# Last inverse stage through ScalarE, shift weights by broadcast, coarser units and a new order in a fused Hyena-like block

## The chip, the cores and the metric

The kernel runs on one core of a Trainium2 chip. Five engines work side by side, each through its own queue in the order in which the program was written: TensorE (PE; its weight loads are shown as PEld), VectorE (DVE), ScalarE (ACT), GpSimd (POOL) and SyncE (SP), which here only issues DMAs. The metric is device time in microseconds (us); lower is better.

## The reference

For 2048 positions of 640 channels the block computes a normalisation, a gated long convolution and a feed-forward net, and joins them:

```python
xn = _layernorm(x)                       # x is A_q, [2048, 640]
k_shift = sum(k_pad[t:t+S] * shift_k[:, 3-t] for t in range(4))
kv = k_shift * v
y = irfft(rfft(kv, 2S) * rfft(ssm_k, 2S))[:S] + kv * ssm_D
s = xn * y
h = gelu(xn @ w1 + b1)                   # 640 -> 1728
g = silu(h @ w2 + b2)                    # 1728 -> 640
out = x + s * g
```

## The kernel before

The 2048 positions lie as 128 partitions by 16 tiles of 640 channels (x, xn, k, v). The convolution is done as a two-stage transform by matmuls, with its results passed through three scratch tensors in DRAM, which turn rows into columns between the stages:

- Forward stage 1 (`stage1`, operations K1, K1r, U1, U1r): the filter K = ssm_k and the signal U = kv, tile by tile, times a table W. `Ke`, `Ker`, `Ue`, `Uer` evict PSUM to a staging buffer `st` of four slots, and `Ks`, `Us` store each slot to scrK or scrU.
- Forward stage 2, in eight groups s: `KLs`, `ULs` load a group from scrK and scrU, K2, U2 and X2 (X2 does the last 128 channels of both) transform it, `Kf`, `Uf` evict, `pr` and `qr` multiply the two spectra.
- Inverse stage 1: `i1`, `i1r`, evicted by `ie`, `ier`, stored to scrC by `cs_0` to `cs_7`.
- Inverse stage 2: `cl_0` to `cl_7` load from scrC (each once all stores are in), `i2_i` makes tile i of y.

The signal comes from the shift convolution `kv` on VectorE: five pieces of rows, each four multiplications with a spread weight row, three additions and one product with v. The spread weights `wx` (4 × 640 values on all 128 partitions) are made in the head.

The feed-forward net runs in four quarters c of four tiles. Each tile is normalised (`bn` statistics, `ep` and `rs` for the reciprocal root, `xn`), then transposed: `xt` on TensorE with eviction `xe` for quarters 0 and 1, a DMA transpose `xT` for 2 and 3. `f1_c_ft_r` makes 128 hidden features for piece r of the quarter, and `ge` applies Gelu while evicting; `f1h`, `geh` do the last 64 features. `f2_i_n` makes half n of tile i's output, `si` evicts it through Silu, `gx` multiplies it into xn. At the end `ym` multiplies y in, `ad` adds x, and `os` stores.

Nothing is scheduled on the chip. `ORDER` is a list of all operations by name; `plan.emit` records them in that order, so it sets the order in every engine's queue. Behind a name, `/P`, `/S`, `/D`, `/A` pick POOL, SP, DVE or ACT where there is a choice, `/C` splits a matmul into two halves of 64 output columns, and the numbers behind a colon are buffer slots: PSUM banks (eight), slots of `st`, and the 11 row blocks of the tile kvl in which the loads of the second stages land. An operation waits until its slot's earlier user is done.

Warm-up matmuls (`warm`) fill TensorE in the head before the first data.

Of the kernel before, what the change touches and what calls it, by code (L numbers as in the profile page):

```python
# [112 lines left out]
def h3_block(ctx: ExitStack, tc: tile.TileContext, x_d, k_d, v_d, sk_d, K_d, D_d, w1_d, b1_d, w2_d, out_d):  # L113
# [33 lines left out]
    ones = sb.tile([1, P], BF16, name="ones")  # L147
# [12 lines left out]
    sk_r = lat_t[0:1, 0:4, :].rearrange("p a d -> p (a d)")  # L160
# [17 lines left out]
    def evict(e, out_, in_):  # L178
        (nc.scalar.copy if e == "ACT" else nc.vector.tensor_copy)(out=out_, in_=in_)  # L179
# [12 lines left out]
    def pair():  # L192
        return Buf(pool=ps, size=2)
# [15 lines left out]
    Fb, Ib, idb, b1b, b1rb, Db, cb, tmb, smb, skb, zb, mhb = (Buf() for _ in range(12))  # L209
# [100 lines left out]
    def load(name, eng, o_, i_, reads=(), writes=()):  # L310
        op(name, eng, lambda e: qu(e).dma_start(out=o_, in_=i_), reads=reads, writes=writes)
# [18 lines left out]
    load("skl", "ACT", sk_r, sk_d, writes=[skb])  # L330
    for j in range(4):
        pb = pair()

        def wx_mm(e, j=j, pb=pb):
            for h in range(2):
                nc.tensor.matmul(out=pb.v[:, h, 0:H], lhsT=ones[:], rhs=sk_r[:, j * D + h * H:j * D + (h + 1) * H],
                                 start=True, stop=True)
# [50 lines left out]
    LG = ((0,), (1,), (2, 3)) + tuple(tuple(range(4 * c, 4 * c + 4)) for c in range(1, NCH))  # L388

    def bn(e, i):  # L390
        for h in range(2):
            nc.vector.bn_stats(out=stats[:, i, h, :], in_=x_t[:, i, h * H:(h + 1) * H])  # L392
        nc.vector.bn_aggr(out=mv[:, i, :], in_=stats[:, i, :, :])
# [8 lines left out]
    for g, tiles in enumerate(LG):  # L402
        for i in tiles:
            op("bn%d" % i, "DVE", lambda e, i=i: bn(e, i), reads=[xb[i]], writes=[mvb[i]])
# [112 lines left out]
    kt = Pool(2, lambda s, n: kvt_t[s], after=[[skb]] * 2)  # L517
# [20 lines left out]
    for i in range(8):  # L538
# [3 lines left out]
              after=[kv_done[0:(2, 3, 4, 5)[m]] for m in range(4)] + [vb[4 * m:4 * m + 4] for m in range(4)] + [acc + wxb + [skb]] * 3)  # L542
    pm = Pool(5, lambda s, n: st_t[:, s * 4 * CA:(s + 1) * 4 * CA], after=[stored] * 5)
    rest = None
    for s in range(NG):
# [41 lines left out]
        prb = [Buf(pool=pm), Buf(pool=pm)]  # L587
        for w in range(2):
# [23 lines left out]
        if s % 2 == 0:  # L612
            rest = dict(b=Buf(pool=pm), p=[Buf() for _ in range(4)], U=[], C=[], s=[])
# [41 lines left out]

    for r in range(NG):
# [3 lines left out]
        for i in (2 * r, 2 * r + 1):  # L660
            pb = pair()

            def i2(e, i=i, b=cb_, pb=pb):
# [6 lines left out]
            op("ym_%d" % i, "DVE", lambda e, i=i, pb=pb: nc.vector.tensor_tensor(  # L670
                out=xn_t[:, i, :], in0=pb.v.rearrange("p a b -> p (a b)")[:, 0:D], in1=xn_t[:, i, :], op=ALU.mult), reads=[pb], writes=xnb[i])
            if i >= FLIP:
                continue
            op("ad_%d" % i, "DVE", lambda e, i=i: nc.vector.tensor_tensor(  # L674
                out=x_t[:, i, :], in0=xn_t[:, i, :], in1=x_t[:, i, :], op=ALU.add), reads=xnb[i], writes=[xb[i]])
            op("os_%d" % i, "SP|ACT", lambda e, i=i: qu(e).dma_start(out=out_d[:, i, :], in_=x_t[:, i, :]), reads=[xb[i]])
# [117 lines left out]
```

## Time and profile before

| what | us |
|---|---|
| median of 3 runs (185.93 to 187.03) | 186.15 |
| the profiled execution | 186.39 |
| its span, first to last instruction | 184.6 |
| TensorE busy | 176.7 |
| VectorE busy | 156.5 |
| ScalarE busy | 144.2 |
| GpSimd busy | 15.3 |

The profile is of one execution, whose own time is 1.8 us longer than its span. Rows of groups read: line, engine, operation, output<-input by the program's names, shapes, count, busy time, mean ns of one. Rows of the timeline and of the chain begin with the start in us and the length. "SPq" or "ACTq" is an engine's queue issuing a DMA. The tile name of an eviction is its output, ps is PSUM.

### The profile page before, as it was taken

To read this page: it belongs to the slowest core of one execution; us is meant where nothing else is said; L and a number is where in the kernel's file an instruction comes from. 1 tells how busy PE (TensorE), PEld (TensorE's weight loads), DVE (VectorE), ACT (ScalarE), POOL (GpSimd) and SP (SyncE) were. 2 spreads that over 40 slices of the span, in tenths; PEclk is the share of its full clock that TensorE was granted. 3 is DMA by queue.
4 is the path that set the end of the run, shared out by engine and by line. 5 is a ranking of instruction groups with operands and counts; after the bars stand their busy time and mean duration, and the time that the engine had idled before them with its cause. 6 is when DMAs were issued, how large, how long until landed. Compare 5 with 4: busy or idle time off the path is not lost.

```text
span 184.6 us, 5181 instructions
## 1 busy us (share of the span) xinstructions
PE 176.7 (96%) x2182; PEld 102.6 (56%) x2183; DVE 156.5 (85%) x267; ACT 144.2 (78%) x227; POOL 15.3 (8%) x42
## 2 busy tenths in 40 slices
PE   7998999999999999998999999999999999899991
PEld 2335784547666556664553435544564555588870
DVE  7999999999999999919999969958889730689993
ACT  4898989999999999987859897898797897501120
POOL 2458600000000000020020000000000000000000
PEclk9999999999999999999999999999999999999999
DMA  5999999959879995989989760899923756995275
GB/s 182 411 417 413 401 417 417 431 223 344 305 274 312 401 396 217 385 253 374 220 261 326 135 162 4 260 376 189 362 74 122 265 185 215 388 344 227 77 270 194
DMA packets 29754, 51.81 MB, mean 281 GB/s; under 512 B 9122, under 2 KB 23843, under 8 KB 29348
## 3 DMA queue, kind: packets, MB, share of 16 engines
q1 hardware_dynamic: 28288, 50.21, 78.7%
q10 hardware_dynamic: 1444, 1.28, 2.1%
q8 instruction: 17, 0.28, 0.6%
q14 instruction: 5, 0.04, 0.1%
HBM read 31.30 MB, written 18.35 MB: 269 GB/s over the span
## 4 chain that ended last, share of the span: by engine, by line
PE 71%; DVE 12%; DMA 12%; ACT 3%; issue 1%; ACTq 0%; SPq 0%; DVEq 0%
PE ps L450 32%; PE ps L486 20%; PE ps L603 5%; PE ps L560 4%; PE ps L358 4%; DMA kvl<-scrC 4%; DVE stats L392 3%; DVE xn L670 3%; DMA kvl<-scrU 2%; DMA scrU<-st 2%; DMA x<-in_x 2%; ACT st L179 2%; PE ps L464 1%; PE ps L635 1%; PE ps L574 1%; DVE x L674 1%
## 5 line engine op out<-in xcount | busy, mean ns | idle before, releaser
L486 PE MATMUL ps<-w,hT 128*128 128x320 bf16 (+4 forms) x588 | 66.1, 295 | 0.0
L450 PE MATMUL ps<-xnT,w 128*128 128x512 bf16 (+5 forms) x515 | 62.2, 321 | 0.1
L486 PEld LDWEIGHTS <-hT 128*128 128x128 bf16 (+2 forms) x588 | 45.1, 103 | 19.8 <-issue 6.5
L179 ACT CAST kvl<-ps 128x1024 bf16<-128x1024 f32 (+3 forms) x53 | 42.1, 841 | 8.2 <-PE ps L560 5.1
L450 PEld LDWEIGHTS <-w 128*64 128x64 bf16 (+1 forms) x515 | 32.1, 105 | 25.1 <-issue 7.8
L454 ACT ACTIVATE hT<-ps,b1f 128x512 bf16<-128x512 f32 (+2 forms) x71 | 37.8, 591 | 3.3 <-PE ps L450 3.1
L179 ACT CAST st<-ps 128x1024 bf16<-128x1024 f32 (+1 forms) x45 | 37.8, 902 | 1.3 <-PE ps L358 1.1
L179 DVE CAST kvl<-ps 128x1024 bf16<-128x1024 f32 (+2 forms) x31 | 25.9, 857 | 7.1 <-ACT hT L454 2.3
L490 ACT ACTIVATE sl<-ps 128x320 bf16<-128x320 f32 (+1 forms) x33 | 14.0, 438 | 20.7 <-PE ps L486 14.6
L670 DVE TENSOR_TENSOR xn<-ps,xn 128x640 bf16<-128x640 f32 x16 | 12.8, 819 | 9.5 <-PE ps L666 9.4
L593 DVE TENSOR_TENSOR st<-kvl 128x2048 bf16<-128x2048 bf16 x16 | 19.1, 1217 | 0.3 <-ACT kvl L179 0.3
L531 DVE TENSOR_TENSOR kvl<-kvl 128x2560 bf16<-128x2560 bf16 (+1 forms) x15 | 18.3, 1223 | 0.4
L528 DVE TENSOR_TENSOR kvl<-kvl 128x2560 bf16<-128x2560 bf16 (+1 forms) x15 | 18.3, 1221 | 0.3
L392 DVE BATCH_NORM_STATS2 stats<-x 128x6 f32<-128x320 bf16 x32 | 13.7, 471 | 4.0 <-DMA x<-in_x 4.0
L697 PE MATMUL ps<-hT 128*128 128x512 bf16 x31 | 9.8, 461 | 1.4 <-DVE hT L223 1.3
L492 DVE TENSOR_TENSOR xn<-xn,sl 128x320 bf16<-128x320 bf16 (+1 forms) x33 | 9.8, 309 | 0.8 <-ACT sl L490 0.8
L560 PE MATMUL ps<-kvl,F 64*32 64x512 bf16 x256 | 10.1, 381 | 0.0
L408 POOL TENSOR_TENSOR rstd<-rstd,mhalf 128x4 f32<-128x4 f32 (+2 forms) x6 | 5.0, 838 | 57.1 <-DVE rstd L406 56.8
L603 PE MATMUL ps<-st,I 32*64 32x512 bf16 x256 | 8.9, 380 | 0.0
L624 DVE TENSOR_TENSOR st<-kvl 128x512 bf16<-128x512 bf16 x16 | 6.5, 416 | 0.8 <-ACT kvl L179 0.8
L666 PE MATMUL ps<-kvl,G 128*64 128x512 bf16 (+1 forms) x64 | 6.1, 301 | 1.0 <-DVE x L674 0.5
L697 PEld LDWEIGHTS <-hT 128*128 128x128 bf16 x32 | 3.1, 111 | 6.3 <-issue 3.2
(76 smaller groups left out, 124.4 us busy)
## 6 DMA issues: line engine op xcount, KB each, us to landing
scrK<-st SPq DMA_DIRECT2D x8, 640.0 KB, 5.2
scrU<-st SPq DMA_DIRECT2D x8, 640.0 KB, 4.5
kvl<-scrK SPq DMA_DIRECT2D x8, 640.0 KB, 6.9
kvl<-scrU SPq DMA_DIRECT2D x8, 640.0 KB, 5.7
scrC<-kvl SPq DMA_DIRECT2D x8, 640.0 KB, 4.0
kvl<-scrC SPq DMA_DIRECT2D x8, 640.0 KB, 7.6
kvl<-in_v SPq DMA_DIRECT2D x4, 640.0 KB, 11.5
w<-in_w SPq DMA_DIRECT2D x2, 1120.0 KB, 8.3
```

The costliest lines, as they stand in the source:

```text
L179: (nc.scalar.copy if e == "ACT" else nc.vector.tensor_copy)(out=out_, in_=in_)
L392: nc.vector.bn_stats(out=stats[:, i, h, :], in_=x_t[:, i, h * H:(h + 1) * H])
L450: nc.tensor.matmul(out=pb.v[us, 0:n], lhsT=w1_t[:, ft, t, us], rhs=xnTb[c].v[:, a:b, t, :], start=(t == 0), stop=(t == DT - 1))
L454: nc.scalar.activation(out=hTb[c].v[:, ft, a * P:b * P], in_=pb.v[:, 0:(b - a) * P], func=ACT.Gelu_apprx_tanh, bias=b1_f[:, ft:ft + 1], sc ...
L486: nc.tensor.matmul(out=pb.v[w * u:w * u + w, 0:b - a], lhsT=hTb[c].v[0:M, ft, q * P + w * u:q * P + w * u + w], rhs=w2_t[0:M, ft, a:b], st ...
L490: op("si_%d_%d" % (i, n), "ACT", lambda e, pb=pb, s_=s_, a=a, b=b: nc.scalar.activation(out=s_.v[:, 0:b - a], in_=pb.v[:, 0:b - a], func=A ...
L528: op("kv%d_%dm" % (r, j), "DVE", lambda e, i=i, n=n, j=j, t=t, wb=wb: nc.vector.tensor_tensor(out=t.v[:, 0:n, :], in0=k_t[:, i + 3 - j:i + ...
L531: op("kv%d_%da" % (r, j), "DVE", lambda e, n=n, t=t, a=a: nc.vector.tensor_tensor(out=a.v[:, 0:n, :], in0=a.v[:, 0:n, :], in1=t.v[:, 0:n, ...
L560: nc.tensor.matmul(out=pb.v[32 * j:32 * j + 32, a, :], lhsT=F2_t[64 * a:64 * a + 64, ri, :], rhs=B.v[64 * a:64 * a + 64, j, 0:CA], start=T ...
L593: nc.vector.tensor_tensor(out=pr.v.rearrange("p (a r c) -> p a r c", a=2, r=2), in0=u, in1=k, op=ALU.mult)
L603: nc.tensor.matmul(out=pb[j // 2].v[64 * a:64 * a + 64, j % 2, :], lhsT=I1_t[32 * j:32 * j + 32, m, :], rhs=o[32 * j:32 * j + 32, a, r, :] ...
L670: op("ym_%d" % i, "DVE", lambda e, i=i, pb=pb: nc.vector.tensor_tensor(out=xn_t[:, i, :], in0=pb.v.rearrange("p a b -> p (a b)")[:, 0:D], ...
```

## The change

Five things change, and with them the whole order.

1. Last inverse stage: `ym` no longer reads PSUM. `ye_i` evicts tile i to a new bf16 buffer `yt` (in the space of `st`, free once all products are used), 13 of the 16 on ScalarE and 3 on VectorE; `ym`, and for the first 12 tiles `ad` and `os`, then work on two tiles at once.
2. Shift weights: the 5 KB load, four pairs of matmuls with a row of ones and four evictions go; one DMA `wl` on SP reads the row once for each of 128 partitions into `wx`.
3. Statistics: `bn` does two tiles, the four half-tile statistics first and the two aggregations behind them. The loads of x in the head become tiles 4-5, 6-7 and 0-3 (the last is issued first).
4. Gelu units: quarter 0 goes from 32 pieces to 13 whole units, quarter 1 from 13 whole units to 7 whole and 12 halves.
5. All eight `cs` stores to scrC are on GpSimd's queue (`/P`) instead of SP's.

```diff
-    for g, (a, b) in enumerate(((0, 1), (1, 2), (2, 4), (4, 8))):
+    for g, (a, b) in enumerate(((4, 6), (6, 8), (0, 4))):
         load("xl%d" % g, "SP", x_t[:, a:b, :], x_d[:, a:b, :], writes=xb[a:b])
...
-    load("skl", "ACT", sk_r, sk_d, writes=[skb])
-    for j in range(4):
...
-        op("wm%d" % j, "PE", wx_mm, reads=[skb, cb], writes=[pb])
-        op("we%d" % j, "ACT|DVE", lambda e, j=j, pb=pb: evict(
-            e, wx_t[:, j, :].rearrange("p (h c) -> p h c", h=2), pb.v[:, :, 0:H]), reads=[pb], writes=[wxb[j]])
+    load("wl", "SP", wx_t[:], sk_d.to_broadcast([P, 4 * D]).rearrange("p (j d) -> p j d", d=D), writes=wxb)
...
     def bn(e, i):
-        for h in range(2):
-            nc.vector.bn_stats(out=stats[:, i, h, :], in_=x_t[:, i, h * H:(h + 1) * H])
-        nc.vector.bn_aggr(out=mv[:, i, :], in_=stats[:, i, :, :])
+        for j in range(i, i + 2):
+            for h in range(2):
+                nc.vector.bn_stats(out=stats[:, j, h, :], in_=x_t[:, j, h * H:(h + 1) * H])
+        for j in range(i, i + 2):
+            nc.vector.bn_aggr(out=mv[:, j, :], in_=stats[:, j, :, :])
...
     def pieces(c, ft):
-        if c > 0:
-            return ((0, 4),)
-        return ((0, 1), (1, 2), (2, 4)) if ft < SPLIT else ((0, 2), (2, 4))
+        return ((0, 2), (2, 4)) if c == 1 and ft < SPLIT else ((0, 4),)
...
+    yt = Pool(8, lambda s, n: st_t[:, s * 2 * D:(s + 1) * 2 * D].rearrange("p (a d) -> p a d", d=D), after=[pmb] * 8)
...
-            op("ym_%d" % i, "DVE", lambda e, i=i, pb=pb: nc.vector.tensor_tensor(
-                out=xn_t[:, i, :], in0=pb.v.rearrange("p a b -> p (a b)")[:, 0:D], in1=xn_t[:, i, :], op=ALU.mult), reads=[pb], writes=xnb[i])
...
+            op("ye_%d" % i, "ACT|DVE", lambda e, i=i, pb=pb: evict(
+                e, yb[i // 2].v[:, i % 2, :], pb.v.rearrange("p a b -> p (a b)")[:, 0:D]), reads=[pb], writes=[yp[i]], hold=[yb[i // 2]])
+        i = 2 * r
+        op("ym_%d" % i, "DVE", lambda e, i=i: nc.vector.tensor_tensor(
+            out=xn_t[:, i:i + 2, :], in0=yb[i // 2].v, in1=xn_t[:, i:i + 2, :], op=ALU.mult),
+           reads=yp[i:i + 2] + [yb[r]], writes=xnb[i] + xnb[i + 1])
...
 ORDER = """
-c0 grid xl2 b1l zz fix warm5:0 skl wq1 bn3 ws1 xl3 mh warm12:1 warm2:0 warm3:1 bn2 bn7 Kl3 bn6 warm14:0 id wm2:2 wm3:0 we2 wm0:4
...
+grid zz xl2 warm11:0 b1l fix Kl2 mh sm0 warm12:1 warm5:0 warm1:1 wq1 warm13:0 xl0 c0 bn2 bn0 ws1 warm15:1 Kl3 warm7:0 xl1 ep2/P
...
 """
```

Where the order moves work shows best on the queues. First SP's queue from the second-stage loads to the end; before:

```order
L548 DMA kvl<-scrU 128x4x640
L650 DMA scrC<-kvl 128x4x640
L548 DMA kvl<-scrU 128x4x640 x2
L547 DMA kvl<-scrK 128x4x640 x2
L496 DMA_TRANSPOSE G<-W 128x16x128
L650 DMA scrC<-kvl 128x4x640 x7
L658 DMA kvl<-scrC 128x2560 x6
L676 DMA out<-x 128x640
L658 DMA kvl<-scrC 128x2560 x2
L676 DMA out<-x 128x640 x5
```

and after the change, from the three loads UL7, UL5 and UL6 on (the two loads of scrK are KL6 and KL7):

```order
L535 DMA kvl<-scrU 128x4x640 x3
L534 DMA kvl<-scrK 128x4x640 x2
L482 DMA_TRANSPOSE G<-W 128x16x128
L650 DMA kvl<-scrC 128x2560 x8
L673 DMA out<-x 128x1280 x3
```

The eight stores to scrC (L650 before) are gone from this queue, and no output store stands between the eight loads of scrC any more. The stores are now the last work of GpSimd's queue, behind the reciprocal roots of the layer norm and the preparation of tables:

```order
L302 MEMSET hT_71 1x512
L298 TENSOR_SCALAR I_83<-I_83 128x192
L394 TENSOR_SCALAR rstd<-mv 128x4
L396 TENSOR_TENSOR rstd<-rstd,mhalf 128x4 x2
L639 DMA scrC<-kvl 128x4x640 x8
```

They left SP's queue for one that issued no DMA before.

On VectorE, the first products of the inverse stage before (ps is PSUM, sl the Silu output):

```order
L670 TENSOR_TENSOR xn<-ps,xn 128x640
L674 TENSOR_TENSOR x<-xn,x 128x640
L670 TENSOR_TENSOR xn<-ps,xn 128x640
L674 TENSOR_TENSOR x<-xn,x 128x640
L670 TENSOR_TENSOR xn<-ps,xn 128x640
L492 TENSOR_TENSOR xn<-xn,sl_80 128x320
```

and after, with the three evictions that VectorE keeps (st is the space that yt uses):

```order
L177 CAST st<-ps 128x640
L478 TENSOR_TENSOR xn<-xn,sl_78 128x320
L478 TENSOR_TENSOR xn<-xn,sl_80 128x320
L177 CAST st<-ps 128x640
L665 TENSOR_TENSOR xn<-st,xn 128x1280
L478 TENSOR_TENSOR xn<-xn,sl_79 128x320
L665 TENSOR_TENSOR xn<-st,xn 128x1280
L177 CAST st<-ps 128x640
```

The products read SBUF and are twice as wide; one in two is gone.

More of the change, by code (lines that the diff above doesn't have):

```diff
@@ L208, in h3_block @@
     Gb = [Buf() for _ in range(2)]
[L209 removed]
+    Fb, Ib, idb, b1b, b1rb, Db, cb, tmb, smb, zb, mhb = (Buf() for _ in range(11))
     wxb = [Buf() for _ in range(4)]
@@ L402, in h3_block @@
     for g, tiles in enumerate(LG):
-        for i in tiles:
-            op("bn%d" % i, "DVE", lambda e, i=i: bn(e, i), reads=[xb[i]], writes=[mvb[i]])
+        for i in tiles[::2]:
+            op("bn%d" % i, "DVE", lambda e, i=i: bn(e, i), reads=xb[i:i + 2], writes=mvb[i:i + 2])
         a, b = tiles[0], tiles[-1] + 1
@@ L612, in h3_block @@
         if s % 2 == 0:
-            rest = dict(b=Buf(pool=pm), p=[Buf() for _ in range(4)], U=[], C=[], s=[])
+            pmb.append(Buf(pool=pm))
+            rest = dict(b=pmb[-1], p=[Buf() for _ in range(4)], U=[], C=[], s=[])
         R = rest
@@ new lines @@
+ge_3_6_0 f1_3_2_0/C:1 ge_2_11_0 pr_3_1:1 ier_3/D ier_2/D gx_2_0 i1r_0:6.2 geh_3 UL6/S:4 ge_3_2_0 ier_1 ier_0 i1_0:4.0 ie_0_1
+pr_3_0:2 cs_2/P i1_3:2.6 ie_0_0/D ie_3_1/D pr_4_0:0 ie_3_0 f2_8_1:0.1 KL6/S:10 X2_5:6 U2_5_1:2 U2_5_0:4 Uf_5_2/D Kf_5_2/D si_8_1
+Uf_5_0 f2_8_0:1.0 U2_6_1:6 Uf_5_1 U2_6_0:2 si_8_0 KL7/S:3 qr_4_0:1 Uf_6_1 K2_6_1:4 pr_4_1:2 Uf_6_0 pr_5_1:3 f2_9_0:0.2 K2_6_0:2
+pr_5_0:4 si_9_0 X2_7:6 Kf_6_1 gx_9_0 Uf_7_2/D Kf_6_0 cs_1/P f2_9_1:1.2 Kf_7_2/D qr_5_1 qr_5_0 gx_8_1 i1_5:2.4 si_9_1 f1_3_10_0/C:0
```

118 lines of the change are left out of this document (54 added, 64 removed).

## Prediction

> **What bounds the kernel now.** I read the busy shares first, then the busy time of each stretch, then the chain of work that ended last, then single rows of the timeline. The first fence has the page's row of shares and four stretches of the span; a stretch's first figure is its length, and each engine's is its busy time in it.
>
> ```profile
> PE 176.7 (96%) x2182; PEld 102.6 (56%) x2183; DVE 156.5 (85%) x267; ACT 144.2 (78%) x227; POOL 15.3 (8%) x42
> 18.20:71.30 53.10, 53.10 (x546) 32.59 (x548) 52.17 (x53) 51.10 (x92) 3.48 (x7) 1.00 0.91 346
> 71.30:84.50 13.20, 12.48 (x158) 7.79 (x159) 8.97 (x25) 11.58 (x17) 1.04 (x1) 1.00 0.91 327
> 84.50:157.20 72.70, 72.58 (x1085) 37.13 (x1086) 56.74 (x91) 61.11 (x89) 1.33 (x2) 1.00 0.76 218
> 157.20:181.00 23.80, 22.38 (x289) 17.83 (x288) 21.39 (x47) 6.15 (x13) 0.00 (x0) 1.00 0.72 263
> ```
>
> TensorE has work from 18.2 to the end of the inverse stage. Up to 71.3 VectorE (52.17 of 53.10) and ScalarE (51.10) are as full; after 84.5 they have room, and after 157.2 ScalarE is nearly idle (6.15 of 23.80) while VectorE is nearly full (21.39). So a saving on VectorE counts only at the end, one on ScalarE hardly anywhere, and one on TensorE everywhere. The granted clock is 1.00 in all of them.
>
> What does a TensorE operation cost? In the chain of waits (start, length, what), groups follow each other without a gap:
>
> ```profile
> 18.19 7.90 PE ps L450 x115
> 84.91 0.43 PE ps L560 x16
> 85.35 2.01 PE ps L486 x14
> 87.36 0.56 PE ps L560 x16
> 154.25 1.90 PE ps L486 x14
> 173.67 6.86 PE L486 MATMUL ps<-w,hT 128*128 128x320 bf16 x56
> ```
>
> Fourteen matmuls of 320 columns take 1.90 beside matmuls of the same tile shape (154.25) and 2.01 between others (85.35); sixteen of the second forward stage take 0.43 behind their like and 0.56 between others. So a change of tile shape costs 0.11 to 0.13, and the rest is columns at about 2,400 a us. The first feed-forward matmul is at 18.19, the last ends at 173.67 + 6.86 = 180.53 (this row is the timeline's): 162.3. Counted from the written order by columns and 0.13 a change, the work in it is 157.6 (145.3 of columns, 95 changes), so 4.7 are waits.
>
> **TensorE's own work.** The new order has 75 changes of shape behind its first feed-forward matmul instead of 95: 20 × 0.13 = 2.6 less. Three transposes of xn now come behind that matmul (3 × 0.33 = 1.0 more) and one forward tile ahead of it (0.2 less). Feed-forward pieces of 128, 256 or 512 columns have the same columns in all. Work: 155.8, **1.8 less**. The eight matmuls that spread the shift weights lay in the head, where TensorE runs warm-up matmuls: nothing.
>
> **The head.** In the chain and the timeline, statistics, normalised tiles and transposed copies precede the matmul at 18.19; the fifth line is the page's row of GB/s, one figure for each 4.6 us.
>
> ```profile
> 4.53 0.90 DVE stats L392 x2
> 6.44 0.21 DVE mv L393
> 6.65 0.76 DVE stats L392 x2
> 13.17 1.02 DVE xn L412 x3
> GB/s 182 411 417 413 401 417 417 431 223 344 305 274 312 401 396 217 385 253 374 220 261 326 135 162 4 260 376 189 362 74 122 265 185 215 388 344 227 77 270 194
> 16.36 1.68 DVE L179 COPY xnT<-ps 128x640 bf16<-128x640 bf16 x4
> ```
>
> One tile's statistics take 0.76 + 0.21, about 1.0, and all eight come ahead of the first xn at 13.17. The first x load grows from 320 to 640 KB; at 411 GB/s that is 0.8 more, so they start at 5.3. Six tiles (three pairs; pairing saves at most the small gaps, I take 5.8) end at 11.1, three xn at 12.1, the fourth pair at 14.0, two xn 14.7, bit operations 15.2, two copies of 0.42 16.05, one small cast and the third copy 16.6. The first whole Gelu unit starts at 16.7 and not 18.19: **1.5 earlier**. The four ScalarE evictions of spread weights that go make room for two more of the copies there.
>
> Whole units also relieve ScalarE: eight Gelu evictions of 256 columns take 3.02, four of 512 take 2.42.
>
> ```profile
> 24.76 3.02 ACT L454 ACTIVATE hT<-ps,b1f 128x256 bf16<-128x256 f32 x8 [0.63 <-PE ps L450]
> 154.29 2.42 ACT L454 ACTIVATE hT<-ps,b1f 128x512 bf16<-128x512 f32 x4 [0.81 <-PE ps L450]
> ```
>
> At 0.38 and 0.60 a piece the first two quarters go from 20 × 0.38 + 12 × 0.31 (the 128s, estimated) + 13 × 0.60 = 19.1 to 20 × 0.60 + 12 × 0.38 = 16.6. These 2.5 hide behind TensorE, which is the one always busy there; I count nothing.
>
> **The shift convolution on VectorE.** It must be done before the last forward tile of U. Two rows of the timeline (first and last of its run), the group that multiplies by the Silu output, and the load of k that starts it:
>
> ```profile
> 20.27 1.47 DVE L528 TENSOR_TENSOR kvl<-kvl 128x2560 bf16<-128x2560 bf16 x1
> 71.59 0.83 DVE L533 TENSOR_TENSOR kvl<-kvl 128x1280 bf16<-128x1280 bf16 x1
> L492 DVE TENSOR_TENSOR xn<-xn,sl 128x320 bf16<-128x320 bf16 x31 | 9.3, 314 | 0.8 <-ACT sl L490 0.8
> 7.68 0.33 SPq L311 DMA_DIRECT2D kvl<-in_k  x1
> kvl<-in_k SPq DMA_DIRECT2D x1, 1120.0 KB, 9.6
> ```
>
> The run is 20.27 to 72.4, or 52.1. The new order puts eight of the multiplications in it instead of five (+0.9) and two pairs of statistics (+3.8), and has one 1.1 eviction less: 55.8 or so. It starts some 0.8 earlier, at 19.5, where TensorE's first unit is 1.5 earlier but three xn follow the copies; it ends at 75.3, plus about 1.0 for two multiplications whose Silu comes late. TensorE wants the tile at 16.7 + 59.4 (its work up to there) = 76.1. **Wait: 0.4**; before it there was none to speak of. The start also hangs on the load of k, which landed at 7.68 + 9.6 = 17.3. The broadcast load puts 640 KB ahead of it, 1.6 at 411 GB/s: 18.9, still before 19.5, with 0.6 to spare. A load that spreads one row over 128 partitions is not in the trace: it may cost nothing (if it fits into gaps) or as much as the slowest 640 KB load quoted below (12.4, k then some 4 late); I take 1.6, the rate row, as it moves the same bytes.
>
> **Stores and loads between the stages.** SP carried all eight stores of the inverse spectrum; now GpSimd's queue does, which issued no DMA in this trace, so the time from issue to landing there, L, is the unknown. Rows of issues, of single operations and of the chain:
>
> ```profile
> scrU<-st SPq DMA_DIRECT2D x8, 640.0 KB, 4.5
> kvl<-scrK SPq DMA_DIRECT2D x8, 640.0 KB, 6.9
> x<-in_ssm_k SPq DMA_DIRECT2D x2, 640.0 KB, 12.4
> L593 DVE TENSOR_TENSOR st<-kvl 128x2048 bf16<-128x2048 bf16 x16 | 19.1, 1217 | 0.3 <-ACT kvl L179 0.3
> L650 SPq DMA_DIRECT2D scrC<-kvl x8: 359/436/1151, 115.1 to 149.4; - x8
> DMA to landing us min/median/max: 3.2/4.0/6.5
> L408 POOL TENSOR_TENSOR rstd<-rstd,mhalf 128x4 f32<-128x4 f32 x3 | 3.1, 1038 | 57.0 <-DVE rstd L406 56.8
> 146.93 1.00 PE ps L603 x32
> 152.72 3.38 SPq L658 DMA_DIRECT2D kvl<-scrC  x6
> 157.24 0.41 PE ps L666 x4
> ```
>
> Bounds for L: 3.2, the fastest of these stores from SP, and 12.4, the slowest transfer of that size. It is nearest to the median store, 4.0; to it I add 1.0, the longest that one plain GpSimd instruction takes here (1038 ns): L = 5.0. Two places feel it.
> - The load KL7 now takes the buffer of the store cs_2. Behind its last eviction VectorE does one multiplication (0.3) and the product (1.2) that lets i1_3 start, so it is ready 1.5 ahead of i1_3. X2_7, which needs KL7, stands 8.9 behind i1_3's start (i1_3 1.0, three half tiles 6.0, second-stage groups 1.9). With 6.0 for KL7 (the median of such loads is 6.9, with others in flight; few are then) TensorE waits L − 4.4, at 5.0 **0.6**.
> - The last store was issued at 149.4, the loads behind it at 152.72 (3.3 later), and TensorE's first inverse matmul at 157.24 started as its load landed. The cover, from the end of i1_7 at 147.93, was 9.3 and is 9.2 now (five units and two half tiles in both orders). So TensorE waits L − 3.3, at 5.0 **1.7**.
>
> Other transfers: U1_12 takes the slot of a store of 4.5 behind 0.7 of eviction, and 3.9 of matmuls cover it: 0 to 1.3, I take **0.6**. K2_6 wants KL6 6.4 behind the product that frees its buffer (i1_3 1.0, two half tiles 4.0, second-stage groups 1.4), and such a load takes 6.9: **0.5**.
>
> [...]
>
> **The end.** The rows are the chain, SP's issues and groups by shape:
>
> ```profile
> 163.51 7.00 DMA kvl<-scrC
> 163.51 0.90 SPq L658 DMA_DIRECT2D kvl<-scrC  x2
> L670 DVE TENSOR_TENSOR xn<-ps,xn 128x640 bf16<-128x640 f32 x16 | 12.8, 819 | 9.5 <-PE ps L666 9.4
> L674 DVE TENSOR_TENSOR x<-xn,x 128x640 bf16<-128x640 bf16 x12 | 5.8, 485 | 0.1
> L179 ACT CAST kvl<-ps 128x640 bf16<-128x640 f32 x4 | 2.7, 720 | 0.5 <-PE ps L336 0.5
> L528 DVE TENSOR_TENSOR kvl<-kvl 128x1280 bf16<-128x1280 bf16 x6 | 4.9, 821 | 0.1
> ```
>
> VectorE: 16 × 0.82 + 12 × 0.49 = 19.0 becomes 8 × 0.82 + 6 × 0.82 + three evictions of about 0.85 = 14.0: 5.0 less. ScalarE gets 13 × 0.72 = 9.4, in a stretch where 17 of its 23.8 are free. The last two loads stood on SP behind an output store until 163.51 and landed 7.00 later, when TensorE waited; now all eight go first. From 157.24 to 180.53 are 23.3, of which 21.2 are work by the count above; of the 2.1 of waits I keep 0.5: **1.6 less**. From the last matmul to the end it was 184.6 − 180.5 = 4.1; VectorE now has two pair operations queued ahead of the last ones, and I take 4.5.
>
> **Sum.** 16.7 + 155.8 + 4.7 = 177.2; + 0.4 + 0.6 + 0.5 + 0.6 + 1.7 − 1.6 = 179.4; + 4.5 = 183.9 against a span of 184.6, 0.7 less. The profiled execution took 186.39, 0.24 above the median of 186.15, so I subtract from the median: **185.5**.
>
> **Rivals.**
> - **Slow stores** (slower). Place: cs_2 ahead of X2_7, and cs_7 ahead of the inverse loads. Price: 2 us per us of L above 4.4. From L = 5.3 it is slower than before, from 6.3 by over 1%; at 7.5 it gives 190.5. [...] 0.28.
> - **Cheap stores** (faster): L = 4.0 or less takes off 1.6 to 2.3, giving 183.2 to 183.9. The median row is for it. 0.24.
> - **The convolution starts late** (the broadcast load holds back k, or VectorE's longer run meets late Silu tiles): every us past 0.6 is one on the path, as U's last tile stands in front of all loads of the second stage; 1 to 4 late gives 186.5 to 189.5. 0.12.
> - That VectorE's 5.0 come off the span as such gives 180.5; the stretch's work on TensorE speaks against it, and I leave it out of the chances.
>
> **How the numbers follow.** Forecast, L from 4.4 to 5.9 and no late convolution: 184.1 to 187.3, chance 0.36. About 1%, or 1.9, is what a measurement of this kernel can tell from no change. Faster by that (under 184.3): cheap stores 0.24 and 0.04 of the forecast, 0.28. Slower (over 188.0): 0.26 of the slow stores, 0.09 of the late convolution, 0.35. Within: 0.37. The range, 182.6 to 190.5, leaves out 0.1 on either side.
>
> **What would show it.** First feed-forward matmul near 16.7; VectorE's convolution to about 76; a wait for kvl<-scrK ahead of X2_7 and for kvl<-scrC ahead of the first inverse matmul, together near 2.3; stores from GpSimd landing in about 5; no wait for kvl<-scrC in the last 20 us. I am wrong if the first matmul is at 18 or later, if stores take over 6, or if TensorE waits for ScalarE where Gelu units and forward evictions mix.

## The result, and the profile after

The changed kernel takes 193.12 us (median of 4 runs, 192.16 to 196.23); the kernel before, run beside it, 186.04. The ratio is **1.037**, 95% interval 1.027 to 1.048: 3.7% slower, where 185.5 was forecast. The profiled execution is the 196.23 one, span 194.4; it ran in a slower state that the ratio leaves out, so the accounts further below rest on a second profile of the same kernel, of an execution of 192.24.

From the page, the shares, the granted clock in 40 slices of 4.9 us, three groups and one row of DMA issues:

```profile
PE 179.1 (92%) x2166; PEld 103.7 (53%) x2166; DVE 149.5 (77%) x251; ACT 149.1 (77%) x227; POOL 21.1 (11%) x48
PEclk9999999999999999996699999999579999999996
L547 PE MATMUL ps<-kvl,F 64*32 64x512 bf16 x256 | 11.3, 409 | 2.9 <-DMA kvl<-scrU 2.9
L639 POOL DMA_DIRECT2D scrC<-kvl x8 | 6.3, 784 | 69.3 <-DMA kvl<-scrU 37.2
L561 PE MATMUL ps<-kvl,F 64*32 64x256 bf16 x128 | 3.7, 306 | 4.7 <-DMA kvl<-scrK 4.7
scrC<-kvl POOLq DMA_DIRECT2D x8, 640.0 KB, 6.1
```

TensorE's share falls from 96% to 92%, and two waits hold nearly all of its new idle time: 2.9 for a load from scrU (UL2, ahead of U2_2_0) and 4.7 for one from scrK (KL7, ahead of X2_7). In the course of each, the clock drops. TensorE's timeline at the two places:

```profile
89.58 1.05 PE L547 MATMUL ps<-kvl,F 64*32 64x512 bf16 x16 [2.89 <-DMA kvl<-scrU]
90.99 3.92 PE L472 MATMUL ps<-w,hT 128*128 128x320 bf16 x14
138.91 0.63 PE L561 MATMUL ps<-kvl,F 64*32 64x256 bf16 x16 [4.75 <-DMA kvl<-scrK]
139.48 3.91 PE L472 MATMUL ps<-w,hT 128*128 128x320 bf16 x14
```

And the two stretches of half clock, to their edges (columns as in the prediction's first fence; the figure of the clock is the third from the end):

```profile
88.84:95.67 6.83, 6.09 (x62) 2.63 (x61) 2.78 (x4) 2.71 (x4) 0.00 (x0) 0.50 0.94 269
136.62:143.45 6.83, 4.54 (x38) 2.18 (x46) 2.52 (x6) 0.02 (x1) 0.00 (x0) 0.50 0.65 100
```

Fourteen matmuls that take 2.0 elsewhere take 3.9 there. At a clock of 0.50, the 6.09 and 4.54 of busy time hold work for half as long: 3.0 and 2.3 are lost on top of the waits of 2.89 and 4.75. That is 12.9 of this execution.

What does X2_7 wait for? In the chain of waits, the store cs_2 and the load KL7, which takes its buffer, stand one behind the other, and later the last store cs_7 ahead of the inverse loads:

```profile
123.56 6.24 DMA scrC<-kvl
129.82 9.05 DMA kvl<-scrK
...
161.17 3.75 DMA scrC<-kvl
```

So the store lands 6.24 after issue and the load another 9.05 later. The last store, beside which no other queue moved anything from 161.1 to 165, takes 3.75.

### The profile page after: what moved, and what is told of

It is laid out like the page before. It is cut to its first block, busy times and chain, and to the rows that moved or that the text cites. A ratio compares the mean times of both kernels' runs of the same rounds, so it can differ in the third digit from the quotient of the medians.

```text
span 194.4 us, 5147 instructions
## 1 busy us (share of the span) xinstructions
PE 179.1 (92%) x2166; PEld 103.7 (53%) x2166; DVE 149.5 (77%) x251; ACT 149.1 (77%) x227; POOL 21.1 (11%) x48
## 3 DMA queue, kind: packets, MB, share of 16 engines
q0 software_dynamic: 1152, 5.24, 8.0%
## 4 chain that ended last, share of the span: by engine, by line
PE 66%; DMA 20%; DVE 9%; issue 2%; ACT 0%; SPq 0%; POOLq 0%; ACTq 0%
PE ps L436 25%; PE ps L472 25%; DMA scrC<-kvl 5%; DMA kvl<-scrK 5%; PE ps L344 3%; DMA kvl<-scrU 3%; DVE stats L379 3%; PE ps L591 3%; PE ps L547 3%; PE ps L658 2%; DMA x<-in_x 2%; DMA scrU<-st 2%; DMA kvl<-scrC 2%; DVE kvl L177 2%; DVE xn L400 1%
## 5 line engine op out<-in xcount | busy, mean ns | idle before, releaser
L472 PE MATMUL ps<-w,hT 128*64 128x320 bf16 (+3 forms) x714 | 69.5, 301 | 0.0
L436 PE MATMUL ps<-xnT,w 128*128 128x512 bf16 (+3 forms) x380 | 60.6, 361 | 0.0
L472 PEld LDWEIGHTS <-hT 128*64 128x64 bf16 (+2 forms) x714 | 49.7, 108 | 18.7 <-issue 6.3
L177 ACT CAST st<-ps 128x1024 bf16<-128x1024 f32 (+2 forms) x59 | 46.4, 848 | 4.9 <-PE ps L658 2.1
L177 ACT CAST kvl<-ps 128x1024 bf16<-128x1024 f32 (+2 forms) x50 | 39.4, 839 | 8.9 <-PE ps L547 6.5
L436 PEld LDWEIGHTS <-w 128*128 128x128 bf16 (+1 forms) x380 | 28.1, 103 | 28.5 <-issue 6.6
L177 DVE CAST kvl<-ps 128x512 bf16<-128x512 f32 (+2 forms) x30 | 25.8, 881 | 22.5 <-PE ps L561 6.0
L440 ACT ACTIVATE hT<-ps,b1f 128x512 bf16<-128x512 f32 (+1 forms) x58 | 34.5, 654 | 3.4 <-PE ps L436 3.0
L476 ACT ACTIVATE sl<-ps 128x320 bf16<-128x320 f32 (+1 forms) x33 | 14.0, 437 | 16.7 <-PE ps L472 14.9
L639 POOL DMA_DIRECT2D scrC<-kvl x8 | 6.3, 784 | 69.3 <-DMA kvl<-scrU 37.2
L177 DVE CAST st<-ps 128x640 bf16<-128x640 f32 (+2 forms) x5 | 4.4, 872 | 10.2 <-PE ps L658 10.2
## 6 DMA issues: line engine op xcount, KB each, us to landing
kvl<-in_v SPq DMA_DIRECT2D x4, 640.0 KB, 12.9
```

What stands on the lines that cost most here:

```text
L436: nc.tensor.matmul(out=pb.v[us, 0:n], lhsT=w1_t[:, ft, t, us], rhs=xnTb[c].v[:, a:b, t, :], start=(t == 0), stop=(t == DT - 1))
L440: nc.scalar.activation(out=hTb[c].v[:, ft, a * P:b * P], in_=pb.v[:, 0:(b - a) * P], func=ACT.Gelu_apprx_tanh, bias=b1_f[:, ft:ft + 1], sc ...
L472: nc.tensor.matmul(out=pb.v[w * u:w * u + w, 0:b - a], lhsT=hTb[c].v[0:M, ft, q * P + w * u:q * P + w * u + w], rhs=w2_t[0:M, ft, a:b], st ...
L476: op("si_%d_%d" % (i, n), "ACT", lambda e, pb=pb, s_=s_, a=a, b=b: nc.scalar.activation(out=s_.v[:, 0:b - a], in_=pb.v[:, 0:b - a], func=A ...
```

## The experiments

Each row of the table is the changed kernel with one edit, unless it says otherwise. Ratios are to the kernel before, run beside it; "KL7" is its time from issue to landing, and the wait is TensorE's at X2_7, both in the profiled execution.

| run | edit | median us | ratio (95%) | KL7 | wait |
|---|---|---|---|---|---|
| c_after | none | 192.12 | 1.035 (1.027 to 1.044) | 9.62 | 4.54 |
| e1_xt2 | xT2 behind UL1 | 195.40 | 1.050 (1.041 to 1.060) | 10.56 | 5.40 |
| e2_gt | G's transposition after KL7 | 193.87 | 1.045 of the medians | 8.77 | 4.00 |
| e3_cssp | all 8 stores on SP | 184.67 | 0.996 (0.992 to 1.001) | at most 6.8 | 0 |
| e4_cs2 | cs_2 on SP | 192.19 | 1.038 (1.031 to 1.045) | 11.18 | 3.75 |
| e5_cs103 | cs_1, cs_0, cs_3 on SP | 187.00 | 1.005 (1.000 to 1.011) | 6.21 | 0.86 |
| e6_first4 | first 4 stores on SP | 184.92 | 0.997 (0.992 to 1.002) | – | 0 |
| e7_fill | both waits filled | 190.45 | 1.026 (1.018 to 1.034) | – | filled |
| e3_again | as e3_cssp | 184.48 | 0.995 (0.990 to 1.000) | – | 0 |
| e8_ym | e3, last stage undone | 186.47 | 1.004 (1.000 to 1.008) | – | 0 |
| e9_best | e3, two half tiles moved | 185.80 | 1.000 (0.995 to 1.004) | – | 0 |
| e10_befP | kernel before, stores on GpSimd | 188.32 | 1.010 (1.004 to 1.015) | – | 0 |
| e11_kl7P | KL7 on GpSimd, ahead of 3 stores | 187.08 | 1.009 (1.005 to 1.014) | 6.18 | 1.72 |
| e12_fill | e3, 1.3 us filled at U2_2_0 | 185.13 | 0.999 (0.994 to 1.003) | 6.59 | 0.23 |
| e13_act | cs_1, cs_0, cs_3 on ScalarE | 189.26 | 1.014 (1.004 to 1.024) | 9.64 | 3.65 |

### Three suspects: the transposing copies, G, and the queue of the stores

The edits are moves in the written order, except one copy on VectorE that holds G back:

```diff
 c_after: no edit
 e1_xt2
- ... xT2:1 f2_4_0:1.2 si_1_1 UL3/S:8 U2_2_0:4 UL1/S:9 ...
+ ... f2_4_0:1.2 si_1_1 UL3/S:8 U2_2_0:4 UL1/S:9 xT2:1 ...
 e2_gt
+ op("wd", "DVE", lambda e: nc.vector.tensor_copy(out=W_t[:, 0, 0:2], in_=W_t[:, 0, 0:2]), writes=Wb)
- ... Uf_7_2/D ... gt ...
+ ... Uf_7_2/D wd gt ...
 e3_cssp
- cs_0/P to cs_7/P
+ cs_0/S to cs_7/S
```

> The changed kernel once more, as the measure for the other three runs. It should again be some 7 us slower than before. If the two stretches of half clock in its profile (88.8 to 95.7 and 137.4 to 142.7 us) follow from TensorE's two waits ahead of them, they come back at the same places; if they were an accident of that one execution, they are gone or stand elsewhere.

> The transposed copy of xn for quarter 2 is issued behind the loads UL3 and UL1 instead of right behind UL2. Theory A (that transposing DMA slows the load UL2 next to it): UL2 lands in about 4.6 us as before the change instead of 6.4, TensorE's wait at X2_2 falls from 2.9 to under 1, no half clock behind it; 3 to 5 us less than the changed kernel. Rival (UL2 is slow through the store Us_7 and the load KL4 beside it): it still lands after 88 us, the wait stays, the time moves by under 1 us. A transposed copy that then comes too late would show as a wait ahead of the first f1_2 of up to 1 us.

> G's transposing DMA is held back until KL7 has landed, by a copy of two columns of W onto themselves on VectorE behind Uf_7_2 (0.1 us there). Theory B (G's transposition makes KL7 slow): KL7 lands in some 6.5 us instead of 9.05, TensorE's wait at X2_7 falls from 4.75 to about 2.2, and the half clock behind it shrinks or goes; 2.5 to 4.5 us less than the changed kernel. Rival (KL7 is late only through the store cs_2 that holds its buffer): KL7 takes 9 us as before, the wait stays, the time moves by under 1 us.

> All eight stores to scrC go back to SP's queue. Theory C (the GpSimd queue makes them slow, 6.1 us median against 4.0 before): cs_2 lands in about 4, KL7 is issued 2.2 us earlier, the wait at X2_7 falls from 4.75 to about 2.5; 2 to 4 us less than the changed kernel. Rival (the store is slow through the traffic and VectorE's work beside it, not through its queue): cs_2 still takes about 6, the time moves by under 1 us. The last store, 3.75 from GpSimd, should take 3.2 to 4.0 from SP, so the first inverse matmul starts no earlier relative to its stage under either.

**c_after.** Both waits come back; the low clock comes back behind the longer one only. TensorE's timeline:

```profile
89.17 0.63 PE L547 MATMUL ps<-kvl,F 64*32 64x512 bf16 x16 [2.39 <-DMA kvl<-scrU]
135.35 0.41 PE L561 MATMUL ps<-kvl,F 64*32 64x256 bf16 x16 [4.54 <-DMA kvl<-scrK]
135.69 3.75 PE L472 MATMUL ps<-w,hT 128*128 128x320 bf16 x14
```

**e1: a miss.** The wait for UL2 falls to 1.16, but the transposed copy, now behind three loads, lands 9.18 after its issue, 6.9 behind UL2, and TensorE waits for it instead (timeline, TensorE):

```profile
88.00 0.63 PE L547 MATMUL ps<-kvl,F 64*32 64x512 bf16 x16 [1.16 <-DMA kvl<-scrU]
94.97 1.25 PE L436 MATMUL ps<-xnT,w 128*128 128x512 bf16 x5 [3.56 <-DMA xnT<-xn]
```

The place where xT2 stands is a trade between two waits, and the changed order has the better of the two.

**e2: a miss.** Without G's transposition beside it KL7 still takes 8.77; the wait is 4.00 and the time does not fall (its two quickest runs, 191.69 and 192.86, lie where c_after's do). G is not the cause.

**e3: the whole loss.** With SP's queue for all stores no wait at X2_7 is left, and the kernel is as fast as the one before. Beside each other, the queues that issue around KL7, first in c_after (GpSimd, then SP; L534 are KL6 and KL7, L482 is G), then in e3 (SP):

```profile
120.32 0.99 POOL L639 DMA_DIRECT2D scrC<-kvl  x1 [33.90 <-DMA kvl<-scrU]
121.48 0.77 POOL L639 DMA_DIRECT2D scrC<-kvl  x1 [0.18 <-ACT kvl L177]
123.35 0.75 POOL L639 DMA_DIRECT2D scrC<-kvl  x1 [1.09 <-DVE kvl L177]
124.74 0.75 POOL L639 DMA_DIRECT2D scrC<-kvl  x1 [0.64 <-DVE kvl L177]
```

```profile
121.22 4.83 SPq L534 DMA_DIRECT2D kvl<-scrK  x2
126.10 8.97 SPq L482 DMA_TRANSPOSE G<-W  x1
```

```profile
118.30 0.36 SPq L639 DMA_DIRECT2D scrC<-kvl  x1
119.74 2.41 SPq L534 DMA_DIRECT2D kvl<-scrK  x2
122.24 0.89 SPq L639 DMA_DIRECT2D scrC<-kvl  x1
123.18 6.94 SPq L482 DMA_TRANSPOSE G<-W  x1
130.22 18.95 SPq L639 DMA_DIRECT2D scrC<-kvl  x6
```

The time from issue to landing of the two scrK loads, KL6 and KL7, in e3:

```profile
DMA to landing us min/median/max: 5.6/6.2/6.8
```

On GpSimd, cs_1, cs_0 and cs_3 are issued as soon as their data are ready, at 121.5, 123.4 and 124.7, ahead of KL7 at 125.7, which waits for cs_2. On SP the written order holds them back: cs_1 comes behind KL7, the others behind G. So two things change at once: cs_2 is later and slower, and three stores of 640 KB overtake KL7.

The rate of the DMAs from 125.5 to 130 agrees: it is 418 GB/s in c_after, where KL7 is under way beside the stores (the highest slice on the page of the kernel before is 431), and 251 in e3. What each queue moved from 127 to 130 in c_after (packets, MB, share of the 16 DMA engines; q0 is GpSimd's, q1 SP's) shows who had that rate:

```profile
q0 software_dynamic: 270, 1.22, 99.8%
q1 hardware_dynamic: 12, 0.02, 1.4%
```

KL7, issued at 125.7, gets next to nothing while the three stores are moved.

### The late store, or the three that overtake?

```diff
 e4_cs2
- cs_2/P
+ cs_2/S
 e5_cs103
- cs_1/P cs_0/P cs_3/P
+ cs_1/S cs_0/S cs_3/S
 e6_first4
- cs_2/P cs_1/P cs_0/P cs_3/P
+ cs_2/S cs_1/S cs_0/S cs_3/S
```

> Only the store cs_2 goes back to SP's queue; the other seven stay on GpSimd's. With all on SP cs_2 was issued at 118.3 and let KL7 go 3.5 us later, and KL7 took some 6; with all on GpSimd cs_2 took 5.4 and KL7, with the stores cs_1, cs_0 and cs_3 issued ahead of it, 9.6. Theory D (two costs: the late and slow cs_2, some 3 us, and the three stores that overtake KL7, some 3 us): KL7 is issued 3 us earlier but still takes 8 to 9 us, TensorE's wait at X2_7 falls from 4.5 to about 1.5, the time lies 2 to 4 us under the changed kernel (ratio to before 1.015 to 1.03). Rival (cs_2's lateness is all): no wait, ratio about 1.00. Rival (the overtaking is all): as the changed kernel, 1.035.

> The stores cs_1, cs_0 and cs_3 go back to SP's queue, where they stand behind KL7; cs_2 and the last four stay on GpSimd's. Theory D: KL7 is issued as late as in the changed kernel but takes about 6 instead of 9.6, the wait at X2_7 falls from 4.5 to about 1.5, ratio to before 1.015 to 1.03. If the overtaking is all, there is no wait and the ratio is about 1.00; if cs_2 is all, KL7 still ends 4.5 late and the ratio stays at 1.035.

> The first four stores (cs_2, cs_1, cs_0, cs_3) go back to SP's queue, the last four stay on GpSimd's. If GpSimd's queue costs nothing at the last place, where TensorE waited 0.4 to 0.5 for the first inverse tile, this is as fast as all eight on SP (184.7, ratio 0.996). If the price of 1.7 of the prediction's sum holds there (last store 5.0 long), it is 1 to 2 us slower than that.

The chains, first e4, then e5:

```profile
119.65 3.53 DMA scrC<-kvl
123.19 11.18 DMA kvl<-scrK
```

```profile
119.30 5.08 DMA scrC<-kvl
124.40 6.21 DMA kvl<-scrK
```

In e4 cs_2 is quick (3.53) and KL7 leaves 2.5 earlier than in c_after, at 123.2 against 125.7, yet lands at 134.4, only 0.9 earlier: the three stores beside it make it 11.18. Here only cs_1 is issued ahead of KL7 (121.35); cs_0 is issued with it (123.23) and cs_3 behind it (124.61), and G follows KL7 on its own queue (123.6). So a store on another queue need not be ahead of a load to hold it up. The ratio stays at 1.038; in part that is the clock, which is at half over 5.1 us of work behind the wait (to 139.5) and over 3.4 in c_after. In e5 cs_2 is as slow as the prediction took it to be (5.08), KL7 takes 6.21, the wait is 0.86 and the ratio 1.005. So **the three stores beside KL7 are nearly the whole price**, and theory D, which gave half to each, is wrong: the rival that named the overtaking alone is nearest. e6 has the same ratio as e3, although TensorE waited 1.41 at its first inverse tile: the last four stores cost nothing measurable on GpSimd's queue.

### Order, or queue?

```diff
 e11_kl7P
- KL7/S:3
+ KL7/P:3
 e13_act
- ... ie_0_1 pr_3_0:2 ... ie_3_0 ... cs_1/P ... cs_0/P ... cs_3/P ...
+ ... ie_0_1 cs_1/A pr_3_0:2 ... ie_3_0 cs_0/A cs_3/A ...
 e10_befP (kernel before)
- cs_0/S to cs_7/S
+ cs_0/P to cs_7/P
```

> The changed kernel with one edit: the load KL7 stands on GpSimd's queue too, behind cs_2 and ahead of cs_1, cs_0 and cs_3, which then have to wait for it there. Theory F (it is the order of the load and the three stores that matters, not which queue holds them): KL7 is issued as late as in the changed kernel but takes 6 to 7 instead of 9.6, the wait at X2_7 falls from 4.5 to about 1 to 2, the ratio to before falls from 1.035 to 1.005 to 1.015. Rival (GpSimd's queue itself is what slows the neighbouring transfers): KL7 still takes 9 or more, the ratio stays at 1.03 or above.

> The changed kernel with the three overtaking stores cs_1, cs_0 and cs_3 on ScalarE's queue, issued there as soon as their data are evicted; cs_2 and the last four stay on GpSimd's. So they still have a queue apart from KL7's and still stand ahead of it in time, but ScalarE's transfers go in packets like SP's: a store on SP's queue made 4224 - in eight - packets of 1.24 KB, the eight on GpSimd's 1152 of 4.55 KB. Theory G (queues take turns by packets, so GpSimd's large packets take most of the rate from KL7): KL7 takes 7 to 8.5 instead of 9.6, the wait at X2_7 falls from 4.5 to 2 to 3.5, ratio to before 1.015 to 1.03. Rival (any store that is issued first goes first): KL7 takes 9 or more, ratio 1.03 or above. ScalarE waits up to 1 us for VectorE's evictions ahead of cs_3, which should move nothing.

> The kernel before with one edit: its eight stores to scrC on GpSimd's queue, in its own order. In its profile SP issued cs_2 at 115.1, then the loads and G's transposition, and the other seven stores only from 128.0. Theory D (stores on a queue of their own overtake the loads KL7 and KL6): they are issued as their data are ready, KL7 or KL6 takes 2 to 4 us longer, TensorE waits at X2_7 or K2_6, and the time grows by 1.5 to 5 us (ratio 1.01 to 1.03). Rival (the price belongs to the new order alone, with cs_2's buffer for KL7): ratio within 0.995 to 1.005.

**e11** keeps every store on GpSimd and puts KL7 ahead of the three in that same queue. GpSimd's timeline and the chain:

```profile
125.19 0.79 POOL L534 DMA_DIRECT2D kvl<-scrK  x1 [5.00 <-DMA scrC<-kvl]
125.96 2.25 POOL L639 DMA_DIRECT2D scrC<-kvl  x3
```

```profile
125.19 6.18 DMA kvl<-scrK
```

KL7 takes 6.18, though it is issued no earlier: 4.5 ahead of the time at which X2_7 could have started, 5.1 in c_after (the start of X2_7 less its wait). The ratio falls from 1.035 to 1.009. Behind KL7 in one queue the three stores do it no harm (6.18 here, 6.21 in e5). It is the order, not GpSimd's queue.

**e13** is not clear. The page counts packets and MB for each queue, here those of c_after (GpSimd's, SP's) and of e3 (SP's):

```profile
q1 hardware_dynamic: 23776, 45.99, 68.9%
q0 software_dynamic: 1152, 5.24, 8.1%
```

```profile
q1 hardware_dynamic: 28000, 51.24, 81.0%
```

So the eight stores go in 1152 packets of 4.55 KB from GpSimd, and in 4224 of 1.24 KB from SP. With three of them on ScalarE's queue, which makes small ones too (926 for 1.15 MB below), KL7 still took 9.64 in the profile (of the slowest of the four executions), as the rival says (chain of waits):

```profile
125.98 9.64 DMA kvl<-scrK
```

But the ratio of 1.014 lies below both ranges, with a wide interval. What the queues moved from 127 to 130 in e13 (q10 is ScalarE's) looks like c_after, though the packets are small:

```profile
q10 hardware_dynamic: 926, 1.15, 103.3%
q1 hardware_dynamic: 28, 0.03, 3.1%
```

Theory G has the queues take turns by packets. From 130 to 133 e13's two queues do move alike, 0.58 and 0.61 MB; from 127 to 130 they do not in either run (926 packets against 28 in e13, 270 against 12 in c_after), although KL7 had been issued at 126.0 and 125.7. So neither turns by packets nor the packets' size accounts for KL7's delay in these rows. Why the stores go first stays open.

**e10** shows when the move is cheap. In the order before, GpSimd issues the same three stores only behind KL7 and KL6 (SP's timeline, then GpSimd's):

```profile
123.24 1.07 SPq L547 DMA_DIRECT2D kvl<-scrK  x2
```

```profile
124.77 2.27 POOL L650 DMA_DIRECT2D scrC<-kvl  x3 [7.12 <-ACT kvl L179]
```

There is no wait at X2_7, where its theory expected one, and the price is 1.0% instead of 3.5 to 4. In this profile none of it lies between the first and the last feed-forward matmul, 162.3 in both kernels: the first starts 1.2 later than before (19.40 against 18.19), ahead of any store, and what follows the last takes 0.9 more (5.0 against 4.1). Whether the edit causes either is not shown.

### Does the wait cost its clock?

```diff
 e7_fill
- WARM = (2,) * 16
+ WARM = (2,) * 16 + (10, 20)
+ nc.tensor.matmul(out=pb.v, lhsT=W_t[:, 0, :], rhs=W_t[:, 0:4, :].rearrange("p a b -> p (a b)"), start=True, stop=True)
- ... U2_2_0:4 ... X2_7:6 ...
+ ... warm16:4 U2_2_0:4 ... warm17:6 X2_7:6 ...
 e12_fill (on e3_cssp)
+ WARM = (2,) * 16 + (6,)
+ ... warm16:4 U2_2_0:4 ...
```

> The changed kernel with matmuls that nobody reads in TensorE's two waits: 10 of 512 columns (2.1 us) ahead of U2_2_0 and 20 (4.3 us) ahead of X2_7, on the table W and into banks that are free there. Theory E (TensorE's clock halves because it stood idle, so each wait is paid again in slow matmuls behind it): the clock stays at 1.00, the half tile behind X2_7 takes 2.0 instead of 3.9, the time falls by 1.5 to 3 us although work is added. Rival (the halved clock is not set off by the wait): the low stretches stay, the time stays or grows by up to 2.

> All stores on SP's queue, and six matmuls of 512 columns that nobody reads (1.3 us) ahead of U2_2_0, where TensorE waits 0.9 to 1.7 for the load UL2. Theory E: the wait now and then sets off a stretch of half clock (runs at a mean clock of 0.984 to 0.986 took 186.2 to 186.4, those at 0.995 and above 183.7 to 185.2); with the wait filled these go, and the median falls by 0.2 to 0.5 us, ratio to before 0.990 to 0.995. Rival (the slower runs come from elsewhere): nothing changes, 0.995 to 0.997.

In e7 the added matmuls take the waits' place, the clock is full in all 40 slices, and the half tile behind X2_7 is back at 2.08:

```profile
PEclk9999999999999999999999999999999999999999
```

```profile
130.72 4.26 PE L695 MATMUL ps<-W 128*128 128x512 bf16 x19 [0.16 <-issue]
134.92 0.41 PE L561 MATMUL ps<-kvl,F 64*32 64x256 bf16 x16
135.26 2.08 PE L472 MATMUL ps<-w,hT 128*128 128x320 bf16 x14
```

All four times (189.93 to 191.01) lie under all of c_after's (191.79 to 193.83), though the two were not measured side by side and the intervals of the ratios overlap. With 30 matmuls more the kernel is some 1.7 us faster. The mean clock of its four runs is 0.994 to 1.000, of c_after's 0.975 to 0.991. So the low clock is set off by the waits. It was 0.50 for 6.83 us twice in the first profile, and for about 3.4 in c_after, where the half tile took 1.67 more (3.75 against 2.08), and in e9 (below). The length of the wait alone does not decide it: 2.89 in the first profile and 1.81 in e9 set the half clock off, while 3.56 in e1, 2.62 in e13 and 2.39 in c_after set nothing off. What else decides is not shown. Full clock came back 6.1 and 4.5 us behind the two waits of the first profile, 3.8 behind c_after's.

e12 is a miss: the clock stayed at 0.994 or above in all twelve runs, as the theory says, but the median did not fall (ratio 0.999 against 0.995, intervals overlapping). Without the filling, in e3 and e3_again, four of 22 runs had a mean clock under 0.99, and they were the four slowest (185.96 to 186.37); with it no run had, yet three of twelve took 186.16 to 186.65. Filling these waits of 1 to 1.7 gained nothing that shows.

### The last stage, and a try at a faster version

```diff
 e8_ym (on e3_cssp)
- op("ye_%d" % i, "ACT|DVE", ... evict(e, yb[i // 2].v[:, i % 2, :], ...))
- op("ym_%d" % i, "DVE", ... two tiles from yt ...)
+ op("yd_%d" % i, "DVE", lambda e, i=i, pb=pb: nc.vector.tensor_tensor(
+     out=xn_t[:, i, :], in0=pb.v.rearrange("p a b -> p (a b)")[:, 0:D], in1=xn_t[:, i, :], op=ALU.mult), reads=[pb], writes=xnb[i])
 e9_best (on e3_cssp)
- ... UL3/S:8 U2_2_0:4 ... gx_1_1 X2_2:6 ... f2_3_1:0.0 ... i2_13:2 ... si_11_1 gx_11_1 f2_12_1/C:4.0 ...
+ ... UL3/S:8 gx_1_1 f2_3_1:0.0 U2_2_0:4 ... X2_2:6 ... si_11_1 gx_11_1 f2_12_1/C:4.0 i2_13:2 ...
```

> The changed kernel with all eight stores on SP's queue once more, as the measure for the next two runs. Ratio to before 0.99 to 1.00, as in its first run (0.9964).

> Stores on SP's queue, and the last inverse stage undone: the product with y reads PSUM on VectorE again, tile by tile, with no eviction by ScalarE; sums and output stores of the first 12 tiles stay in pairs. By the prediction's step on the end (1.6 of waits less, 0.4 more behind the last matmul) this is 1.2 us slower than the kernel with SP's stores, and VectorE is busy some 3 us longer after the first inverse matmul. Rival (TensorE sets the stage in both): no difference beyond 0.5 us.

> Stores on SP's queue, and two half tiles of feed-forward moved ahead of TensorE's two waits for loads: f2_3_1 ahead of U2_2_0 (wait 1.0 in the profile with SP's stores, up to 2.9 in others) and f2_12_1 ahead of the first inverse tile (wait 0.2 and 0.9). Theory: both waits go, 1 to 2.5 us less than the kernel with SP's stores, ratio to before 0.985 to 0.992. Rival (the loads behind are late by as much, or the tail grows by what is moved out of it): no difference.

**e8** is 2.0 us slower than e3_again, where 1.2 was expected, so the eviction by ScalarE is worth that. With the product on PSUM, TensorE waits for it (timeline of e8; L662 is the product):

```profile
170.38 0.46 PE L658 MATMUL ps<-kvl,G 128*64 128x512 bf16 x4 [1.47 <-DVE xn L662]
```

**e9** filled both waits and met two new ones, this one and 0.92 for an eviction in the last stage:

```profile
91.19 0.62 PE L547 MATMUL ps<-kvl,F 64*32 64x512 bf16 x16 [1.81 <-ACT kvl L177]
```

The half tile had also covered an eviction behind it. The wait of 1.81 sets off the half clock, from 91.8 to 95.2, and the four of e9's twelve runs with a mean clock under 0.99 are its four slowest (186.74 to 187.37). No version clearly beats the kernel before; e3_cssp, at 0.996 and 0.995, comes nearest, and its intervals just reach 1.

## Why the prediction was wrong

Step by step, as the prediction put them:

- **The head**, 16.7: right. The first feed-forward matmul is at 16.38 in the first profile (16.47 in c_after).
- **TensorE's own work**, 1.8 less: about right. In e3 it runs from 16.39 to the end of this row, 177.87, so 161.5, of which 2.1 are waits:

```profile
172.90 4.97 PE L472 MATMUL ps<-w,hT 128*64 128x320 bf16 x84
```

  That leaves 159.4; the 162.3 of before hold 1.7 of waits, 160.6 without them. The gain is 1.2. So of the 4.7 that the prediction called waits, 3.0 were work that its count by columns missed; it carried the 4.7 over whole, so the sum did not suffer.
- **The convolution**, to end at 75.3 to 76.3: right. VectorE's last piece ends at 75.8, and TensorE does not wait (0.4 was taken; the prediction's own 76.3 and 76.1 give 0.2):

```profile
74.99 0.83 DVE L519 TENSOR_TENSOR kvl<-kvl 128x1280 bf16<-128x1280 bf16 x1
```

- **Stores and loads**: here the prediction failed, in one term, the 6.0 for KL7. The unknown L was taken as 5.0 and is 5.1 to 6.2 for cs_2: near. But in "with 6.0 for KL7 (the median of such loads is 6.9, with others in flight; few are then)" the bracket is false. At L = 5.35 (c_after) the sum gives a wait of 1.0; it was 4.54, and the 3.6 between are KL7's 9.62 less 6.0. The prediction listed what waits for the moved stores and forgot what they had waited behind. SP's timeline of the kernel before:

```profile
118.99 1.02 SPq L547 DMA_DIRECT2D kvl<-scrK  x2
120.06 7.81 SPq L496 DMA_TRANSPOSE G<-W  x1
127.99 21.74 SPq L650 DMA_DIRECT2D scrC<-kvl  x7
```

  SP's queue had kept seven of them behind KL7, KL6 and G's transposition, to 127.99. With a queue of their own they need nothing but their data. That moving them past SP's loads sends them ahead of those, or beside them, was there to be read in the order, and was not read. e5 and e11 show it: the same slow store with the old sequence costs 0.5 to 0.9%.
- **A wait's second price**: absent from the sum. The half tile behind X2_7 took 3.75 instead of 2.08 (c_after), 1.7 more, and 2.3 were lost there in the first profile; e7 shows that this follows from the wait.
- **The load UL2**: no wait beyond before's 0.7 was foreseen; it was 0.90 to 2.89 in profiles of kernels that are alike up to there. Neither its spread nor its mean is explained; e1 only shows that xT2 cannot simply move.
- **The last store**, wait L − 3.3: the formula was right, L too high. At 3.75 it gives 0.45; measured 0.51 in the first profile and 0.42 in c_after.
- **U1_12 (0.6) and K2_6 (0.5)**: neither wait appeared.
- **The end**, 1.6 of waits less within the stage and 0.4 more behind it: wrong against the kernel before. Its timeline has 1.0 of waits inside the stage (0.54, 0.23 and 0.19), not 2.1, and e3 still has 0.95. Against the new order without the eviction the 1.6 is there: e8 waits 2.53 in the stage (1.06 and 1.47). Behind the last matmul e3 takes 4.7, 0.6 more than before.

Against e3, measured beside it, c_after's loss is 7.45 in medians. The two profiles account for 4.54 at X2_7, 1.7 of slow matmuls behind it, 2.39 − 0.99 = 1.4 at U2_2_0, less 1.10 − 0.42 = 0.7 at the inverse tiles: 6.9. The 1.4 may be chance.

Of the rivals, "slow stores" named the right buffer and gave the wrong mechanism: its price hung on L, and e4, where L is 3.5, is as slow as the changed kernel. "Cheap stores" is what e3 amounts to, with 0.8 less than the kernel before where 2.3 to 2.9 less were forecast for it; most of what is missing is the 1.6 of the end. (The forecast's low bound, 184.1 at L = 4.4, is 184.3 by the prediction's own terms.)

## What to carry to other kernels

A queue is also an order: before moving a transfer to another queue, list what it stood behind in the old one, because it will now run as soon as its data are ready, ahead of or beside loads that matter more. Here three stores went out at 121.5, 123.4 and 124.7, as their data came, and KL7 took 9.62 (c_after) instead of 6.21 (e5). If the new queue is wanted, put the load that must go first into it too, ahead of the others (6.18 in e11). Count on a long TensorE wait being paid twice: each of the waits from 3.65 to 5.40 us in these profiles was followed by slow matmuls, of those between 1.8 and 3.6 some were (1.81, 2.89) and some were not (2.39, 2.62, 3.56), and it cost 1.4 (e13) to 3.0 us (the first profile) more.

## What the hardware showed beside that

A load of 640 KB took 6.2 us with three stores of 640 KB held behind it (e5), 9.6 with them issued in the 4 us ahead of it on another queue (c_after), and 11.2 with one of them ahead of it, two at its side and G's transposition right behind it (e4). While the stores were moved at 1.22 MB in 3 us, the load's queue moved 0.02 MB (c_after). TensorE's half clock (0.50) lasted 6.83 us at both places in the first profile and about 3.4 in c_after and e9. Issuing a store occupied GpSimd for 0.75 to 0.99 us (c_after) and SP's queue for as little as 0.36 (e3). Thirty matmuls that nobody reads made a kernel about 1.7 us faster (190.45 against 192.12).
